# Sliding-window attention and two mixing layers on one core: the order of the weight conversion steps at the start is rearranged

## The chip, the cores and the metric

The kernel runs on one NeuronCore of a Trainium2 chip, in one launch. The core has five engines with a queue of their own: PE (TensorE, matrix products), DVE (VectorE), ACT (ScalarE), POOL (GpSimd) and SP (SyncE, which here only issues DMAs). Each works its queue in order; where an instruction waits, everything behind it on that engine waits too. The metric is the device time of one execution in microseconds.

## What is computed

Four sequences of 576 tokens, eight heads of 64. Attention looks back over 64 positions; its output goes through a gated layer (`w_in`, a product over the tokens with `w_spatial`, `w_out`) and through a second pair of layers.

```python
mask = (rel >= 0) & (rel < 64)
scores = where(mask, (q @ k.T) / 8, -1e9)
attn = softmax(scores);  x = attn @ v
h = maximum(x @ w_in, 0);  u, v = h[..., :512], h[..., 512:]
v_n = (v - mean(v)) / sqrt(var(v) + 1e-6)
gated = u * (w_spatial @ v_n + b_spatial[:, None])
x = gated @ w_out
u = x + token_mlp(x);  out = u + channel_mlp(u)
```

## The kernel before

All matrix products of the layers are made from operands split into a high and a low part (`xh`, `xl`; `wi_h`, `wi_l`), three matmuls for each pair. The weights come as 64-bit floats and are turned into 32-bit ones on the chip. A block of 128 x 512 weights takes one DMA of 512 KB into `U` (used as a landing place), one ACT step (Abs, L85 or L391) into `val`, four DVE steps (`to_f32`, L58, L60, L61, L62), one ACT step for the high part (L91 or L397) and one subtraction for the low part: on DVE (L93) for the four blocks `wv` of the second half of `w_in`, on POOL (L399) for the four blocks `wu` of its first half. These blocks are Python generators: each call `go(w)` issues the next step of that block, so that the place of a call in the text is the place of the step in the queues.

The first stage is a loop over 18 iterations (two pairs of sequences, nine tiles of 128 queries each). For tile n: `scores` (PE: mask and q·k, L201 and L206), `smax` (DVE: maxima L217 and their negative, L223, twice), `sexp` (ACT: eight exponentials, L228), `snorm` (DVE: sums to factors and one product for each half, L234, L235, L237, twice), `att_turn` (PE transposes L245, ACT copies to `PT`, L246), `att_pv` (PE, L257; ACT L265 and DVE L266 split the result to `xh`, `xl`). Then `uv_v` multiplies a tile by the second half of `w_in` (PE, L136) and `normalise` follows in turns (ACT L311, DVE L315, L316, L320, POOL L317, L318; then L296 or L288 on ACT, L297 or L289 on DVE). After every third tile four `uv_u` multiply by the first half, one block `wu` each; they are done in iteration 3 for the first time. The text of this part sets the order on every engine, by hand.

Before the loop, tile 0 and the scores of tiles 1 and 2 are interleaved with the steps of the four `wv` blocks. In the loop, `conv` says which `wu` blocks are converted in an iteration: block 0 in iteration 1, block 1 in iteration 2, blocks 2 and 3 in iteration 3. In an iteration the Abs comes behind the transposes, the DVE steps behind `att_pv`, the high part behind the maxima of tile n+2, the low part after that.

Of the kernel before, what the change touches and what calls it, by code (L numbers as in the profile page):

```python
# [29 lines left out]
def f(ap):  # L30
    return ap.bitcast(F32)
# [3 lines left out]
def tile_kernel(ctx, tc, qT, kT, kE, v, w_in, wsT, b_sp, w_out, w_t1, w_t2, w_c1, w_c2, mask, outT):  # L35
# [122 lines left out]
    def where(p, i):  # L158

        return (2 * p + (i - 1) // 4, (i - 1) % 4) if i else (None, None)  # L160

    def load_qk(n):
        p, i = its[n]
        qq = att.tile([P, 4, 128], F32, tag="qq", name="qq")
        nc.sync.dma_start(out=qq.rearrange("p j t -> p (j t)"), in_=qT[n])
        kk = att.tile([P, 4, 256], F32, tag="kk", name="kk")
        if i:
            nc.sync.dma_start(out=kk.rearrange("p j k -> p (j k)")[:, :768], in_=kT[8 * p + i - 1])
            kk = kk.rearrange("p j k -> p (j k)")[:, :768].rearrange("p (j k) -> p j k", k=192)
        else:  # L170
            nc.sync.dma_start(out=kk.rearrange("p j k -> p (j k)"), in_=kE[p])
        held[n] = (qq, kk)
# [14 lines left out]
    def scores(n):  # L187

        p, i = its[n]
        if n >= len(its):
            return
        qq, kk = held.pop(n)
        step = 64 if i else 128
        which = 1 if i and where(p, i)[1] == 0 else 0
        on_pe = n < MASK_PE
        scs = [psa.tile([P, 4, 128], F32, tag="sp", name="sc") for _ in range(2)]
        if on_pe:
            for sc in scs:  # L200
                nc.tensor.matmul(sc, ident16, msk16[:, which].unsqueeze(1).to_broadcast([P, 4, 128]), start=True, stop=False)  # L201
        for j in range(4):
            for q in range(2):
                for e in range(2):
                    er = slice(64 * e, 64 * e + 64)
                    nc.tensor.matmul(scs[e][64 * q:64 * q + 64, j, :], qq[er, j, 64 * q:64 * q + 64],  # L206
                                     kk[er, j, step * q:step * q + 128], start=not on_pe, stop=not on_pe or j == 3)
        pb = att.tile([P, 8, 128], F32, tag="pb", name="pb", bufs=3)
        nm = att.tile([P, 8], F32, tag="nm", name="nm", bufs=3)
        sm = att.tile([P, 8], F32, tag="sm", name="sm", bufs=3)  # L210
        soft[n] = (scs, pb, nm, sm, None if on_pe else msk[:, which])

    def smax(n, g):
        scs, pb, nm, sm, mk = soft[n]
        mx = att.tile([P, 4], F32, tag="mx", name="mx", bufs=3)
        if mk is None:
            nc.vector.tensor_reduce(out=mx, in_=scs[g], op=ALU.max, axis=AX.X)  # L217
        else:
            for h in range(4):
                nc.vector.tensor_tensor_reduce(  # L220
                    out=pb[:, 4 * g + h, :], in0=scs[g][:, h, :], in1=mk, scale=1.0, scalar=-3e38,
                    op0=ALU.add, op1=ALU.max, accum_out=mx[:, h:h + 1])
        nc.vector.tensor_scalar(out=nm[:, 4 * g:4 * g + 4], in0=mx, scalar1=-SCALE, scalar2=None, op0=ALU.mult)  # L223

    def sexp(n, g):
        scs, pb, nm, sm, mk = soft[n]
        for h in range(4 * g, 4 * g + 4):
            nc.scalar.activation(out=pb[:, h, :], in_=scs[g][:, h - 4 * g, :] if mk is None else pb[:, h, :],  # L228
                                 func=AF.Exp, scale=SCALE, bias=nm[:, h:h + 1], accum_out=sm[:, h:h + 1])

    def snorm(n, g):
        pb, sm = soft[n][1], soft[n][3]
        rs = att.tile([P, 4], F32, tag="rs", name="rs", bufs=4)
        nc.vector.tensor_scalar(out=rs, in0=sm[:, 4 * g:4 * g + 4], scalar1=1e-9, scalar2=None, op0=ALU.add)  # L234
        nc.vector.reciprocal(out=rs, in_=rs)  # L235
        half = pb[:, 4 * g:4 * g + 4, :]
        nc.vector.tensor_tensor(out=half, in0=half, in1=rs.unsqueeze(2).to_broadcast([P, 4, 128]), op=ALU.mult)  # L237
# [92 lines left out]
    def tick():  # L330
        for t in list(turns):
            if next(t, turns) is turns:
                turns.remove(t)
# [21 lines left out]
    def run_work(n):  # L355
        used = 0
        for _ in range(min(n, len(work))):
            fn, *a = work.pop(0)
            fn(*a)
            used += COST[fn]  # L360
        return used
# [9 lines left out]
    def wi(js, k, at):  # L371

        return split_steps(wi_h[:, k, js], wi_l[:, k, js], w_in[128 * k:128 * k + 128, js],
                           raw=U[:, k, at:at + 1024], val=stage.tile([P, 2 * WN], F32, tag="raw", name="val"))
# [9 lines left out]
    def wu_part(ft):  # L384
        fs = slice(128 * ft, 128 * ft + 128)
        raw = U[:, ft, :1024].bitcast(I32)
        val = stage.tile([P, 2 * WN], F32, tag="raw", name="val")
        nc.sync.dma_start(out=raw.rearrange("p (k c) -> p k c", k=4), in_=w_in[:, fs].rearrange("(k p) c -> p k c", p=P).bitcast(I32))
        yield
        r3 = raw.rearrange("p (n w) -> p n w", w=2)  # L390
        nc.scalar.activation(out=val, in_=f(r3[:, :, 1]), func=AF.Abs)  # L391
        yield
        to_f32(val, r3[:, :, 0], r3[:, :, 1])
        yield
        hi, lo = wi_h[:, :, fs], wi_l[:, :, fs]
        v3 = val.rearrange("p (k c) -> p k c", k=4)
        nc.scalar.copy(out=hi, in_=v3)  # L397
        yield
        nc.gpsimd.tensor_tensor(out=lo, in0=v3, in1=f(hi), op=ALU.subtract)  # L399

    E = mybir.EngineType
    with tc.manual_schedule(engines={E.PE, E.SP, E.Activation, E.DVE, E.Pool}):
        vs_ = slice(512, 1024)
        load_qk(0)
        nc.sync.dma_start(out=msk, in_=mask)
        nc.gpsimd.tensor_copy(out=msk16, in_=msk)
        wv = [wi(vs_, k, 1152) for k in range(4)]
        wu = [wu_part(ft) for ft in range(4)]

        def go(w):  # L410
            next(w, 0)

        go(wv[0])
        load_v(0)
        go(wv[1])
        load_qk(1)
        go(wv[2])
        scores(0)
        smax(0, 0)
        smax(0, 1)  # L420
        sexp(0, 0)
        go(wv[0])
        sexp(0, 1)
        go(wv[0])
        go(wv[1])
        snorm(0, 0)
        snorm(0, 1)
        go(wv[0])
        go(wv[3])
        load_v(1)  # L430
        load_qk(2)
        scores(1)
        PT = att_turn(0)
        go(wv[1])
        go(wv[0])
        go(wv[2])
        smax(1, 0)
        smax(1, 1)
        att_pv(0, PT)
        go(wv[1])  # L440
        go(wv[2])
        go(wv[1])
        go(wv[3])
        sexp(1, 0)
        go(wv[2])
        go(wv[3])
        go(wv[2])
        go(wv[3])
        go(wv[3])
        sexp(1, 1)  # L450
        go(wu[0])
        load_v(2)
        load_qk(3)
        go(wu[1])
        load_v(3)
        go(wu[2])
        go(wu[3])
        nc.sync.dma_start(out=bb, in_=bass.AP(b_sp.tensor, b_sp.offset, [[0, P], [1, S]]))
        scores(2)
        uv_v(*its[0])  # L460
        snorm(1, 0)
        snorm(1, 1)
        smax(2, 0)
        smax(2, 1)
        conv = {1: (0,), 2: (1,), 3: (2, 3)}
        ws_at = {3: 2, 4: 3, 5: 3, 6: 2}
        for n in range(1, len(its)):
            more, some = n + 2 < len(its), n + 1 < len(its)
            cv = [wu[i] for i in conv.get(n, ())]
            if more and n > 1:  # L470
                load_qk(n + 2)
                load_v(n + 2)
            PT = att_turn(n)
            for w in cv:
                go(w)
            if some:
                sexp(n + 1, 0)
                sexp(n + 1, 1)
                snorm(n + 1, 0)
                snorm(n + 1, 1)  # L480
            tick()
            left = BUDGET - run_work(1)
            att_pv(n, PT)
            for w in cv:
                go(w)
            if more:
                scores(n + 2)
                smax(n + 2, 0)
                smax(n + 2, 1)
            for w in cv:  # L490
                go(w)
            tick()
            for w in cv:
                go(w)
            while work and left > 0:
                left -= run_work(1)
                tick()
            load_ws(ws_at.get(n, 0))
            enable(n)
        while turns:  # L500
            tick()
# [242 lines left out]
```

## Time and profile before

| what | us |
|---|---|
| median of 3 runs | 690.02 |
| lowest and highest run | 688.22 and 690.04 |
| the profiled execution | 689.61 |
| its span in the trace | 687.8 |
| PE busy in the span | 651.5 (95%) |
| DVE, ACT, POOL busy | 358.4, 250.4, 21.7 |

All times in the rows are microseconds from the start of the span. "Idle before" is time in which the engine had nothing running just before an instruction, and the arrow names what ended it.

### The profile page before, as it was taken

Reading aid. Unit: us, or ns where it says so; the run is one execution under the profiler, and the core shown is the slowest. Engines: PE = TensorE matmul, PEld = TensorE weight load, DVE = VectorE, ACT = ScalarE, POOL = GpSimd, SP = SyncE. Lnnn points to the kernel's source line nnn. Section 1 sums busy time; section 2 is a strip of 40 time slices with the busy share of each in tenths; the row PEclk is TensorE's granted clock in tenths of the full one; section 3 lists DMA queues with packets and bytes.
Section 4 is the critical chain, followed back from the end, with each engine's and each line's share of the span. In section 5 each row is a group of like instructions: output and inputs, shape, how many; then the busy total and the mean of one; then the engine's idle time right before and its main releaser. Section 6 shows DMA issues by size and latency. Waiting matters only on the chain.

```text
span 687.8 us, 11757 instructions
## 1 busy us (share of the span) xinstructions
PE 651.5 (95%) x4756; PEld 615.3 (89%) x4756; DVE 358.4 (52%) x913; ACT 250.4 (36%) x675; POOL 21.7 (3%) x49
## 2 busy tenths in 40 slices
PE   3687989999999999999999999999999999999997
PEld 2455769899979999999999998999999999999997
DVE  3878687667675689952389799312212212112112
ACT  3564664552685263752353255111111111111110
POOL 0002100000100010000000000000000000000000
PEclk8689999999999999999999999999999999999999
DMA  8461455223241033200044143100100100100001
GB/s 316 128 210 50 139 170 179 73 75 127 76 139 32 2 106 116 77 1 1 1 153 123 62 155 121 47 1 0 47 1 1 46 1 7 41 1 30 17 1 46
DMA packets 28533, 50.23 MB, mean 73 GB/s; under 512 B 2496, under 2 KB 15168, under 8 KB 28480
## 3 DMA queue, kind: packets, MB, share of 16 engines
q1 hardware_dynamic: 28480, 49.49, 22.0%
q8 instruction: 37, 0.61, 0.4%
q14 instruction: 16, 0.13, 0.1%
HBM read 44.76 MB, written 4.72 MB: 72 GB/s over the span
## 4 chain that ended last, share of the span: by engine, by line
PE 81%; DVE 7%; ACT 7%; DMA 3%; issue 1%; POOL 0%; SPq 0%; DVEq 0%; ACTq 0%
PE mm L136 50%; PE A L647 21%; PE A L136 4%; ACT pb L228 4%; PE xo L257 2%; PE pt L245 2%; PE A L557 1%; ACT PT L246 1%; PE sc L206 1%; DMA raw<-in_wsT 1%; DVE pb L237 1%; DVE val L61 1%; DVE val L62 1%; DVE xl L266 1%; DVE st L315 1%
## 5 line engine op out<-in xcount | busy, mean ns | idle before, releaser
L637 DVE SCALAR_TENSOR_TENSOR g3l<-mm,g3h 128x384 fp32r<-128x384 f32 x72 | 40.0, 556 | 190.3 <-ACT g3h L636 190.1
L636 ACT ACTIVATE g3h<-mm 128x384 fp32r<-128x384 f32 x72 | 35.3, 492 | 223.1 <-PE mm L136 222.6
L136 PE MATMUL mm<-uh,c1h 128*128 128x384 f32 x288 | 97.0, 337 | 1.0 <-ACT c1h L125 1.0
L647 PE MATMUL A<-g3h,c2l 128*128 128x384 f32 x288 | 97.0, 337 | 0.0
L136 PE MATMUL mm<-uh,c1l 128*128 128x384 f32 x288 | 96.7, 336 | 0.1
L136 PE MATMUL mm<-ul,c1h 128*128 128x384 f32 x288 | 96.7, 336 | 0.0
L647 PE MATMUL A<-g3l,c2h 128*128 128x384 f32 x288 | 94.1, 337 | 0.0
L647 PE MATMUL A<-g3h,c2h 128*128 128x384 f32 x288 | 93.8, 337 | 0.0
L136 PEld LDWEIGHTS mm<-uh,c1h 128*128 128x128 f32 x288 | 54.0, 188 | 1.6 <-ACT c1h L125 1.6
L136 PEld LDWEIGHTS mm<-uh,c1l 128*128 128x128 f32 x288 | 54.0, 188 | 0.5 <-DVE c1l L126 0.5
L647 PEld LDWEIGHTS A<-g3h,c2l 128*128 128x128 f32 x288 | 54.0, 187 | 0.2
L136 PEld LDWEIGHTS mm<-ul,c1h 128*128 128x128 f32 x288 | 54.0, 188 | 0.0
L647 PEld LDWEIGHTS A<-g3h,c2h 128*128 128x128 f32 x288 | 53.7, 187 | 0.4 <-ACT c2h L125 0.3
L647 PEld LDWEIGHTS A<-g3l,c2h 128*128 128x128 f32 x288 | 53.8, 188 | 0.0
L136 PE MATMUL mm<-ws_h,nh 128*128 128x288 f32 x160 | 47.5, 301 | 0.9 <-DVE tmp L348 0.9
L136 PE MATMUL mm<-ws_l,nh 128*128 128x288 f32 x160 | 46.4, 295 | 0.0
L228 ACT ACTIVATE pb<-pb,nm 128x128 f32<-128x128 f32 x96 | 37.2, 397 | 2.6 <-DVE nm L223 2.5
L136 PE MATMUL mm<-gh,wo_h 128*128 128x288 f32 x128 | 38.0, 298 | 0.0
L136 PE MATMUL mm<-gh,wo_l 128*128 128x288 f32 x128 | 37.8, 296 | 0.0
L136 PE MATMUL mm<-ws_h,nl 128*128 128x288 f32 x128 | 37.8, 295 | 0.0
L136 PE MATMUL mm<-gl,wo_h 128*128 128x288 f32 x128 | 37.7, 295 | 0.0
L136 PE MATMUL mm<-xh,wi_h 128*128 128x384 f32 x96 | 33.4, 348 | 2.9 <-ACT wi_h L397 2.9
(118 smaller groups left out, 1339.3 us busy)
## 6 DMA issues: line engine op xcount, KB each, us to landing
wraw<-in_w_c SPq DMA_DIRECT2D x24, 512.0 KB, 3.5
kk<-in_kT SPq DMA_DIRECT2D x16, 384.0 KB, 5.0
qq<-in_qT SPq DMA_DIRECT2D x18, 256.0 KB, 4.1
va<-in_v SPq DMA_DIRECT2D x18, 256.0 KB, 2.8
vb<-in_v SPq DMA_DIRECT2D x18, 256.0 KB, 3.7
outT<-ot SPq DMA_DIRECT2D x24, 192.0 KB, 2.1
U<-in_w_in SPq DMA_DIRECT2D x8, 512.0 KB, 7.3
raw<-in_w_out SPq DMA_DIRECT2D x8, 256.0 KB, 3.3
```

The lines of the kernel that those rows point to most:

```text
L61: nc.vector.scalar_tensor_tensor(out=xi, in0=high, scalar=-0x40000000, in1=xi, op0=ALU.bitwise_and, op1=ALU.bitwise_or)
L62: nc.vector.scalar_tensor_tensor(out=xi, in0=low, scalar=29, in1=xi, op0=ALU.logical_shift_right, op1=ALU.bitwise_or)
L136: nc.tensor.matmul(o, a, c, start=(i == 0), stop=(i == n - 1))
L206: nc.tensor.matmul(scs[e][64 * q:64 * q + 64, j, :], qq[er, j, 64 * q:64 * q + 64], kk[er, j, step * q:step * q + 128], start=not on_pe, s ...
L228: nc.scalar.activation(out=pb[:, h, :], in_=scs[g][:, h - 4 * g, :] if mk is None else pb[:, h, :], func=AF.Exp, scale=SCALE, bias=nm[:, h ...
L237: nc.vector.tensor_tensor(out=half, in0=half, in1=rs.unsqueeze(2).to_broadcast([P, 4, 128]), op=ALU.mult)
L245: nc.tensor.transpose(pt[:, h, :], pb[:, 4 * g + h, :], ident)
L246: nc.scalar.copy(out=PT[:, 4 * g:4 * g + 4, :], in_=pt)
L257: nc.tensor.matmul(xo[64 * e:64 * e + 64, j, 64 * q:64 * q + 64], vt[q][:, hc], PT[:, 4 * e + j, 64 * q:64 * q + 64], start=True, stop=True)
L636: nc.scalar.activation(out=gh, in_=ps[:, :CW], func=AF.Relu)
L637: nc.vector.scalar_tensor_tensor(out=gl, in0=ps[:, :CW], scalar=0.0, in1=f(gh), op0=ALU.max, op1=ALU.subtract)
L647: nc.tensor.matmul(acc[d][:, :CW], a, c, start=(ft == 0 and i == 0), stop=(ft == 11 and i == 2))
```

## The change

The transfer of the first `wv` block is issued ahead of the first queries and keys. Its Abs, DVE steps and high part stand ahead of the first scores. The steps of the other `wv` blocks are put behind maxima and ahead of exponentials or normalisations. In the loop, blocks 1 and 2 of `wu` are converted in iteration 2 and block 3 in iteration 3; the first block of an iteration has its DVE steps ahead of the next tile's exponentials in the text (so ahead of its normalisation on DVE) and its high part behind them; the second one has its DVE steps behind `att_pv`.

```diff
+        wv = [wi(vs_, k, 1152) for k in range(4)]
+        wu = [wu_part(ft) for ft in range(4)]
+        go(wv[0])
         load_qk(0)
         nc.sync.dma_start(out=msk, in_=mask)
         nc.gpsimd.tensor_copy(out=msk16, in_=msk)
-        go(wv[0])
+        go(wv[1])
         load_v(0)
-        go(wv[1])
         load_qk(1)
         go(wv[2])
+        go(wv[3])
+        go(wv[0])
+        go(wv[0])
+        go(wv[0])
         scores(0)
         smax(0, 0)
         smax(0, 1)
+        go(wv[1])
+        go(wv[0])
         sexp(0, 0)
-        go(wv[0])
         sexp(0, 1)
-        go(wv[0])
         go(wv[1])
         snorm(0, 0)
         snorm(0, 1)
...
-        conv = {1: (0,), 2: (1,), 3: (2, 3)}
+        conv = {1: (0,), 2: (1, 2), 3: (3,)}
...
             PT = att_turn(n)
-            for w in cv:
-                go(w)
+            go(*cv)
+            go(*cv[:1])
             if some:
                 sexp(n + 1, 0)
                 sexp(n + 1, 1)
                 snorm(n + 1, 0)
                 snorm(n + 1, 1)
+            go(*cv[:1])
             tick()
             left = BUDGET - run_work(1)
             att_pv(n, PT)
-            for w in cv:
-                go(w)
+            go(*cv[:1])
+            go(*cv[1:])
+            go(*cv[1:])
             if more:
                 scores(n + 2)
                 smax(n + 2, 0)
                 smax(n + 2, 1)
-            for w in cv:
-                go(w)
             tick()
-            for w in cv:
-                go(w)
+            go(*cv[1:])
```

On ACT at the start of the program (a row with + is of the new order, with - of the old one, without a sign of both; L85 is an Abs of a `wv` block, L91 its high part, L228 an exponential, L246 the copy of `PT`):

```order
-L228 ACT_TABLE_LOAD
+L85 ACT_TABLE_LOAD
+L85 ACTIVATE val<-U 128x512
+L91 CAST wi_h<-val 128x512
+L85 ACTIVATE val<-U 128x512
+L228 ACTIVATE pb,sm<-sc,nm 128x128 x8
+L85 ACTIVATE val<-U 128x512
+L91 CAST wi_h<-val 128x512
+L246 COPY PT<-pt 128x512 x2
+L85 ACTIVATE val<-U 128x512
 L228 ACTIVATE pb,sm<-sc,nm 128x128 x4
```

The table load stands first, and two Abs stand ahead of the first exponentials, which are eight in a row now; before, the load stood with the exponentials and one Abs between their halves.

On DVE at the start, the rows behind the first block's four steps (maxima of tile 0, the first block's low part, the second block's four steps):

```order
+L217 TENSOR_REDUCE mx<-sc 128x4
+L223 TENSOR_SCALAR nm<-mx 128x4
+L217 TENSOR_REDUCE mx<-sc 128x4
+L223 TENSOR_SCALAR nm<-mx 128x4
+L93 TENSOR_TENSOR wi_l<-val,wi_h 128x512
 L58 TENSOR_SCALAR val<-val 128x512
 L60 TENSOR_SCALAR val<-val 128x512
 L61 SCALAR_TENSOR_TENSOR val<-U,val 128x512
 L62 SCALAR_TENSOR_TENSOR val<-U,val 128x512
```

These four steps stood behind the normalisation of tile 0; they now stand ahead of it.

On DVE in iteration 1 (L58 to L62 convert `wu` block 0; L234, L235, L237 normalise tile 2):

```order
-L320 TENSOR_SCALAR vf<-vf,mv,rstd 128x512
-L266 TENSOR_TENSOR xl<-xo,xh 128x4x128
 L58 TENSOR_SCALAR val<-val 128x512
 L60 TENSOR_SCALAR val<-val 128x512
 L61 SCALAR_TENSOR_TENSOR val<-U,val 128x512
 L62 SCALAR_TENSOR_TENSOR val<-U,val 128x512
+L234 TENSOR_SCALAR rs<-sm 128x4
+L235 RECIPROCAL rs<-rs 128x4
+L237 TENSOR_TENSOR pb<-pb,rs 128x512
+L234 TENSOR_SCALAR rs<-sm 128x4
+L235 RECIPROCAL rs<-rs 128x4
+L237 TENSOR_TENSOR pb<-pb,rs 128x512
```

The conversion has moved from behind `xl` to ahead of the normalisation.

On ACT in iterations 2 and 3 (L391 is an Abs of a `wu` block, L397 its high part, L311 and L265 as above):

```order
+L391 ACTIVATE val<-U 128x512 x2
+L228 ACTIVATE pb,sm<-sc,nm 128x128 x8
+L397 CAST wi_h<-val 128x4x128
+L311 ACTIVATE vf<-mm 128x512
+L265 CAST xh<-xo 128x4x128
+L397 CAST wi_h<-val 128x4x128
+L246 COPY PT<-pt 128x512 x2
 L391 ACTIVATE val<-U 128x512
 L228 ACTIVATE pb,sm<-sc,nm 128x128 x8
-L311 ACTIVATE vf<-mm 128x512
-L265 CAST xh<-xo 128x4x128
-L397 CAST wi_h<-val 128x4x128
```

Iteration 2 has two Abs and two high parts now, and the second high part stands ahead of the copies of iteration 3; one block is left for iteration 3. PE's order is the same in both programs.

## Rows read from the trace of the kernel before

**Rows 1.** The page, part 1: busy time, share, instructions.

```profile
PE 651.5 (95%) x4756; PEld 615.3 (89%) x4756; DVE 358.4 (52%) x913; ACT 250.4 (36%) x675; POOL 21.7 (3%) x49
```

**Rows 2.** Stretches, L136 alone: length, PE busy (count), PEld, PEclk, DMA, GB/s.

```profile
58.80:63.00 4.20, 4.20 (x24) 4.09 (x24) 1.00 0.40 140
67.46:71.30 3.84, 3.84 (x13) 3.84 (x14) 0.56 0.70 201
71.40:73.10 1.70, 1.70 (x10) 1.42 (x9) 1.00 0.03 13
```

**Rows 3.** Timeline, iteration 3: start, duration, engine, operation, [idle before, releaser].

```profile
66.11 0.44 PE L136 MATMUL mm<-xh,wi_h 128*128 128x384 f32 x1 [2.90 <-ACT wi_h L397]
66.13 1.27 POOL L399 TENSOR_TENSOR wi_l<-val,wi_h 128x512 fp32r<-128x512 f32 x1 [2.59 <-ACT wi_h L397]
66.24 1.72 DVE L61 SCALAR_TENSOR_TENSOR val<-U,val 128x512 int32<-128x512 int32 x1
67.46 0.44 PE L136 MATMUL mm<-xh,wi_l 128*128 128x384 f32 x1 [0.73 <-POOL wi_l L399]
```

**Rows 4.** Timeline, start of the program (all engines but PE).

```profile
5.34 0.40 POOL L406 CAST msk<-msk 128x256 bf16<-128x256 f32 x1 [3.69 <-DMA msk<-in_mask]
8.77 0.69 DVE L217 TENSOR_REDUCE mx<-sc 128x4 f32<-128x512 f32 x1 [8.77 <-PE sc L206]
9.74 1.28 ACT L228 ACT_TABLE_LOAD   x1 [9.74 <-DVE nm L223]
13.12 0.43 DVE L58 TENSOR_SCALAR val<-val 128x512 f32<-128x512 f32 x1 [2.66 <-ACT val L85]
15.38 0.16 DVE L234 TENSOR_SCALAR rs<-sm 128x4 f32<-128x4 f32 x1
17.41 0.42 DVE L58 TENSOR_SCALAR val<-val 128x512 f32<-128x512 f32 x1
22.03 0.69 DVE L266 TENSOR_TENSOR xl<-xo,xh 128x512 fp32r<-128x512 f32 x1
27.74 1.46 DVE L93 TENSOR_TENSOR wi_l<-val,wi_h 128x512 fp32r<-128x512 f32 x2
```

**Rows 5.** DMA, the issue at 2.10 alone (first `wv` block): count, KB, us to landing.

```profile
U<-in_w_in SPq DMA_DIRECT2D x1, 512.0 KB, 6.6
```

**Rows 6.** A stretch: PE, PEld, DVE, ACT, POOL busy, PEclk, DMA, GB/s.

```profile
11.00:12.00 1.00, 0.00 (x0) 0.00 (x0) 0.00 (x0) 0.99 (x7) 0.00 (x0) 1.00 1.06 431
```

**Rows 7.** DMA, first issue from 38.12 on alone (block 2 of `wu`).

```profile
U<-in_w_in SPq DMA_DIRECT2D x1, 512.0 KB, 6.0
```

**Rows 8.** Timeline, iterations 1 and 2, DVE, ACT and POOL.

```profile
35.32 0.67 ACT L391 ACTIVATE val<-U 128x512 f32<-128x512 f32 x1
37.41 0.17 DVE L234 TENSOR_SCALAR rs<-sm 128x4 f32<-128x4 f32 x1 [2.24 <-ACT pb L228]
38.62 0.63 ACT L265 CAST xh<-xo 128x512 fp32r<-128x512 f32 x1
39.84 0.54 DVE L320 TENSOR_SCALAR vf<-vf,mv,rstd 128x512 f32<-128x512 f32 x1
43.26 0.62 ACT L397 CAST wi_h<-val 128x512 fp32r<-128x512 f32 x1 [4.00 <-DVE val L62]
43.95 1.26 POOL L399 TENSOR_TENSOR wi_l<-val,wi_h 128x512 fp32r<-128x512 f32 x1 [10.97 <-ACT wi_h L397]
44.65 0.59 DVE L223 TENSOR_SCALAR nm<-mx 128x4 f32<-128x4 f32 x1
45.06 1.07 ACT L246 COPY PT<-pt 128x512 f32<-128x512 f32 x2
50.71 0.69 DVE L315 BATCH_NORM_STATS2 st<-vf 128x6 f32<-128x512 f32 x1
52.10 0.42 DVE L58 TENSOR_SCALAR val<-val 128x512 f32<-128x512 f32 x1
54.99 1.06 ACT L246 COPY PT<-pt 128x512 f32<-128x512 f32 x2
```

More of the change, by code (lines that the diff above doesn't have):

```diff
@@ L403, in tile_kernel, with go @@
         vs_ = slice(512, 1024)
+        wv = [wi(vs_, k, 1152) for k in range(4)]
+        wu = [wu_part(ft) for ft in range(4)]
+        def go(*ws):
+            for w in ws:
+                next(w, 0)
+        go(wv[0])
         load_qk(0)
@@ L406, in tile_kernel @@
         nc.gpsimd.tensor_copy(out=msk16, in_=msk)
[L407 to L411, printed above, removed]
-        go(wv[0])
+        go(wv[1])
         load_v(0)
-        go(wv[1])
         load_qk(1)
         go(wv[2])
+        go(wv[3])
+        go(wv[0])
+        go(wv[0])
+        go(wv[0])
         scores(0)
@@ L427, in tile_kernel @@
         snorm(0, 1)
-        go(wv[0])
-        go(wv[3])
+        go(wv[2])
+        go(wv[1])
         load_v(1)
         load_qk(2)
+        go(wu[0])
         scores(1)
         PT = att_turn(0)
-        go(wv[1])
-        go(wv[0])
-        go(wv[2])
         smax(1, 0)
         smax(1, 1)
+        go(wv[2])
+        go(wv[3])
+        sexp(1, 0)
         att_pv(0, PT)
@@ L441, in tile_kernel @@
         go(wv[2])
[L442 to L445, printed above, removed]
         go(wv[3])
         go(wv[2])
+        sexp(1, 1)
         go(wv[3])
         go(wv[3])
-        sexp(1, 1)
-        go(wu[0])
         load_v(2)
```

## The prediction, made before the changed kernel ran

> **What bounds the kernel now.** I read the page first: PE is busy for 651.5 of 687.8 us [rows 1], so a change that leaves PE's work and its order alone can win at most the 36 us in which PE waits, and what PE loses at its lower clock. The stretches of PE and the timeline say where that is: before about 75 us, in the part that this change rearranges. The largest wait there stands in iteration 3. PE runs the first two `uv_u` at 4.20/24 = 0.175 us a matmul with a granted clock of 1.00 (the upper level, 2.4 GHz), then waits 2.90 us for the high part of `wu` block 2 and 0.73 us for its low part [rows 2, 3]. Behind that wait the granted clock is 0.56 for 3.84 us, mostly the lower level of 1.2 GHz, in which 13 matmuls take 0.295 us each; then it is 1.00 again, with ten in 1.70 us [rows 2]. The waits and the slow matmuls belong together. The last `uv_u` ends at about 73.1, so the question is how early the four `uv_u` end. Ahead of them DVE sets the pace: it converts weights and normalises with few pauses from 13.12 on.
>
> **The start.** The mask's landing releases the first scores now (its cast at 5.34, the first maximum at 8.77) [rows 4]. With the 512 KB block in front, the mask becomes the last of the same four transfers of which the block is the last now, landing at 2.10 + 6.6 = 8.7 [rows 5]. As a lower bound, 512 KB at the 431 GB/s of an undisturbed stretch take 1.2 us [rows 6], so 6.5. I take 8.7, whose row is of these very four, and keep 6.5 for the range. The first maximum then moves by 8.7 - 5.3 = 3.4 us, to 12.2.
>
> Against that stand three savings. The table load of 1.28 us waited for the first negative maxima [rows 4]; it stands first on ACT now, with nothing to wait for. DVE's 2.66 us of idle time ahead of its first conversion go, since at 12.2 work is waiting. And that conversion, 15.38 - 13.12 = 2.26 us, lies ahead of the first maximum, under the transfers. From 8.77 to the last steps on `wv` at 27.74 DVE takes 18.97 us; less 2.66 and 2.26 that is 14.05, which from 12.2 gives 26.25. One wait is new. `xl` comes 22.03 - 15.38 = 6.65 us behind the start of the normalisation (through transposes, `PT`, `att_pv`). The normalisation starts at 12.2 + 2.2 (the maxima and one subtraction: what is left of 22.03 - 17.41 after a conversion, less a small wait) + 2.26, so `xl` at 23.3; DVE gets there some 0.7 us earlier. That makes 26.95: the start gains 0.8 us.
>
> **Iteration 1.** All is 0.8 earlier. The conversion of block 0 moves into DVE's 2.24 us of idle time ahead of the normalisation of tile 2 [rows 8]. Its Abs ends at about 35.9 - 0.8 = 35.1, so the normalisation starts at 37.35 where 36.6 would have done; its first half takes 1.0 and ends at 38.4. By then ACT, behind the last exponential (38.62 - 0.8 = 37.8), makes the high part, and POOL starts its L399 0.69 later (43.95 - 43.26), at 38.5, for 1.27 us [rows 8].
>
> Here is a cost that the diff does not show. Where L399 met DVE in the old order, DVE's instruction stood still until L399 ended: L223 took 0.59 instead of 0.17, L61 1.72 instead of its usual 0.69 [rows 3, 8]. In the new order L399 meets the second half of a normalisation, three instructions on SBUF. That costs nothing if they slip through, 1.2 us if they stand until 39.8; both observed collisions say the second, so the half ends at 40.6 instead of 39.4. The Trainium skill ("SBUF — State Buffer", section "Who interferes with whom") says that DVE and GpSimd share a port pair as an exclusive lock: a DVE instruction with two SBUF inputs, or in a two-port mode, and a GpSimd one that reads SBUF shut each other out, whichever starts first running to its end. L61's 1.72 agrees with it. By that rule the reciprocal (0.2) could pass, and the two collisions that I count would take 0.4 less: 682.9.
>
> L320 and `xl` (1.05), the maxima (1.6) and L297 (two of 0.7, like L266 [rows 4]) follow without the conversion between them: 44.6. ACT, which stands behind the high part until 43.26 now, starts the copies of `PT` for tile 2 at 42.3 (L320, then two casts) instead of 45.06 [rows 8].
>
> **Iteration 2.** Block 1 converts while the exponentials run: 44.6 to 46.85. The normalisation's first half takes 1.0, the second meets L399 again (in the same place as in iteration 1) and ends at 50.1. Then 52.10 - 50.71 = 1.4 to the next conversion, at 51.5 instead of 52.10 [rows 8]. So the copies for tile 3 start at 54.4 instead of 54.99: 0.6 is left. Block 2's transfer lands now at 38.12 + 6.0 = 44.1 [rows 7], 0.8 earlier then; its Abs comes at about 43.9 and just finds it.
>
> **Iteration 3.** `uv_u` starts 0.6 earlier too, at 58.2. Block 2 is ready. Block 3 follows the maxima (done at 55.6) and L320 on DVE, 56.1 to 58.4; its high part stands behind the exponentials, and L399 ends by 61. Its matmuls come up at 58.2 + 36 x 0.175 = 64.5: covered by 3.5 us. 48 matmuls at 0.175 and 0.2 for the last one's end make 8.6 us: 66.8, against 73.1. In terms: 0.6 + 3.6 (both waits) + 2.1 (24 matmuls in 6.3 us now, 4.2 then) = 6.3 us. Nothing behind it is altered: PE's queue, ACT's chain, and the DMAs, which are issued as buffers come free, move along.
>
> So 689.6 - 6.3 = 683.3 us. The sum is made against the profiled execution (689.61, span 687.8); the median 690.02 lies 0.4 above that, inside what the three runs differ by.
>
> **Rivals.**
> - More is won. If L399 holds no instruction of DVE, neither half is 1.2 late, and the gain is 6.3 + 2.4 = 8.7: 680.9. For it: one POOL instruction has to get in between many short ones. Against it: L399 held DVE in both rows. If the mask lands at 6.5, that gives 2.2 as well: 681.1. Both together 678.7. Chance 0.27 for either.
> - A wait for a block comes back. "u weights in the second iteration" is true of two blocks of four only; block 3 stays in iteration 3, and PE waits again if DVE gets to it 3.5 us late. Or block 2's transfer lands late, with next to no cover: ACT then holds the exponentials of tile 3 behind its Abs. If half of the 5.7 us returns, 686.2; 685 to 688. Chance 0.14.
> - Slower: PE's lower clock, in the `uv_u` of iteration 3 and the `uv_v` behind them. PE waits less there, but is still partly idle ahead of them, and its clock did fall after a wait. Taking the full-speed part out of the 3.84 us, a matmul costs 0.325 at the lower level, 0.15 more. All 48 cost 7.2 us, the twelve longer ones of `uv_v` at least 1.8: 692.3. It decides from 42 slow matmuls (6.3/0.15), some 13.7 us at a stretch. Against it: the one after the present wait lasted under 3.84, and 58.80 to 63.00 has 1.00 [rows 2]. Chance 0.05.
> - No change: something behind iteration 3 keeps its old time, and PE waits there instead. Against it: each transfer of the loop is issued behind a PE step that moves. 689 to 690. Chance 0.04.
>
> **How the numbers follow.** The forecast, with 681.3 to 685 as its own range, has 0.50; the rivals as given. A difference under 0.3% (2.1 us) is about what a measurement of this kernel can't tell from no change. Faster by more than that are the forecast, the first rival and most of the second: 0.87. Within it 0.08, slower 0.05. To hold the time 8 times in 10 the range takes in the first rival but for its end and half of the second: 679.2 to 686.5.
>
> **What would show it.** Right: a table load within the first 2 us; the first maximum near 12; copies of `PT` for tiles 2 and 3 near 42.3 and 54.4; DVE instructions of a normalisation that last over 1 us beside L399; four `uv_u` with no wait for `wi_h`, ending near 67; and the same distance kept in all later stages. Wrong in the start, if the first maximum is late and the last steps on `wv` are not before 27.7; wrong in the collision, if `uv_u` ends by 65; wrong in the whole, if PE waits for block 3, or if the gain at 73 is gone at 120.

## The result and the profile after

| | before | after |
|---|---|---|
| median of 4 runs each, us | 689.87 | 681.99 |
| lowest and highest run | 688.22, 690.04 | 681.54, 683.86 |
| profiled execution, its span | 689.61, 687.8 | 682.27, 680.2 |

The ratio is 0.9896, with a 95% interval of 0.9872 to 0.9920. The change makes the kernel 1.0% faster; forecast were 683.3 us, with 679.2 to 686.5 as the range. A second comparison of the same two programs gave 681.65 us and 0.9867 (0.9840 to 0.9895).

The page, part 1, of the kernel after (against [rows 1]):

```profile
PE 649.1 (95%) x4756; PEld 613.8 (90%) x4756; DVE 359.0 (53%) x913; ACT 250.6 (37%) x675; POOL 21.7 (3%) x49
```

The counts are the old ones; PE is 2.4 us less busy, and the span is 7.6 us shorter. So some 5 us of the gain are waits that are gone.

**The start.** The timeline of the kernel after, ACT, DVE and POOL, in order of time (against [rows 4]; L414 is the mask's cast that stood on L406):

```profile
0.72 1.28 ACT L85 ACT_TABLE_LOAD   x1 [0.72 <-PEq L731]
5.76 0.43 DVE L58 TENSOR_SCALAR val<-val 128x512 f32<-128x512 f32 x1 [5.76 <-ACT val L85]
7.95 0.41 POOL L414 CAST msk<-msk 128x256 bf16<-128x256 f32 x1 [6.30 <-DMA msk<-in_mask]
11.39 0.69 DVE L217 TENSOR_REDUCE mx<-sc 128x4 f32<-128x512 f32 x1 [3.29 <-PE sc L206]
15.84 0.16 DVE L234 TENSOR_SCALAR rs<-sm 128x4 f32<-128x4 f32 x1
22.49 0.69 DVE L266 TENSOR_TENSOR xl<-xo,xh 128x512 fp32r<-128x512 f32 x1 [0.69 <-ACT xh L265]
25.95 1.46 DVE L93 TENSOR_TENSOR wi_l<-val,wi_h 128x512 fp32r<-128x512 f32 x2
```

The table load runs under the transfers. The first conversion runs from 5.76, also under them, and DVE still waits 3.29 us for the mask's way to the first maximum. From there on it has work without a pause but for the 0.69 us at `xl`. The last steps on `wv` stand at 25.95 instead of 27.74: 1.8 us earlier.

**Iterations 1 and 2.** The same timeline, DVE, ACT and POOL (against [rows 8]):

```profile
36.84 0.69 DVE L237 TENSOR_TENSOR pb<-pb,rs 128x512 f32<-128x512 f32 x1
37.51 1.27 POOL L399 TENSOR_TENSOR wi_l<-val,wi_h 128x512 fp32r<-128x512 f32 x1 [6.32 <-ACT wi_h L397]
37.65 0.18 DVE L235 RECIPROCAL rs<-rs 128x4 f32<-128x4 f32 x1
37.86 1.48 DVE L237 TENSOR_TENSOR pb<-pb,rs 128x512 f32<-128x512 f32 x1
41.11 1.07 ACT L246 COPY PT<-pt 128x512 f32<-128x512 f32 x2
46.08 0.66 ACT L397 CAST wi_h<-val 128x512 fp32r<-128x512 f32 x1
48.74 0.22 POOL L317 TENSOR_SCALAR rstd<-mv 128x1 f32<-128x1 f32 x1 [9.96 <-DVE mv L316]
49.05 0.57 POOL L318 TENSOR_TENSOR rstd<-rstd,mhalf 128x1 f32<-128x1 f32 x1
49.59 1.29 POOL L399 TENSOR_TENSOR wi_l<-val,wi_h 128x512 fp32r<-128x512 f32 x1
49.60 1.56 DVE L60 TENSOR_SCALAR val<-val 128x512 int32<-128x512 int32 x1
52.65 0.62 ACT L397 CAST wi_h<-val 128x512 fp32r<-128x512 f32 x1 [4.94 <-DVE val L62]
53.17 1.07 ACT L246 COPY PT<-pt 128x512 f32<-128x512 f32 x2
53.33 0.68 DVE L217 TENSOR_REDUCE mx<-sc 128x4 f32<-128x512 f32 x1
53.34 1.27 POOL L399 TENSOR_TENSOR wi_l<-val,wi_h 128x512 fp32r<-128x512 f32 x1 [2.47 <-ACT wi_h L397]
54.05 0.59 DVE L223 TENSOR_SCALAR nm<-mx 128x4 f32<-128x4 f32 x1
```

Read each L399 with the DVE instruction that overlaps it. The first holds the second L237 (1.48 where the first L237 took 0.69, so 0.8 lost), but lets the reciprocal at 37.65 through. The second stands behind L317 and L318 in POOL's queue, of which L317 waits for DVE; it starts at 49.59 and holds L60 of the next block (1.56 where L60 takes 0.43 elsewhere, so 1.1 lost). The third lets the maximum through and holds the small L223. The copies for tiles 2 and 3 stand at 41.11 and 53.17, forecast at 42.3 and 54.4.

**Iteration 3.** PE's timeline, the first and the last matmul of the four `uv_u` of the kernel after:

```profile
58.25 0.67 PE L136 MATMUL mm<-xh,wi_h 128*128 128x384 f32 x1
66.74 0.34 PE L136 MATMUL mm<-xh,wi_l 128*128 128x384 f32 x1
```

The same two of the kernel before:

```profile
58.76 0.44 PE L136 MATMUL mm<-xh,wi_h 128*128 128x384 f32 x1
72.80 0.33 PE L136 MATMUL mm<-xh,wi_l 128*128 128x384 f32 x1
```

After, no wait stands in the 48 rows from one to the other; the last ends at 67.08, where it ended at 73.13. L136 alone, as in [rows 2]:

```profile
58.80:67.00 8.20, 8.20 (x48) 7.96 (x46) 1.00 0.37 132
```

So the waits of 2.90 and 0.73 us are gone [rows 3], and with them the slow matmuls behind them. But the clock fell elsewhere. A stretch of the kernel after, all engines (PE, PEld, DVE, ACT, POOL busy, PEclk, DMA, GB/s):

```profile
55.36:58.77 3.41, 3.41 (x38) 2.24 (x37) 3.17 (x10) 3.41 (x17) 0.00 (x0) 0.50 0.58 112
```

It holds the scores of tile 5 and the first `uv_u` matmuls. In the kernel before, a stretch of about that length holds the same scores, with `att_pv` in front of them:

```profile
55.62:58.83 3.21, 3.05 (x67) 2.25 (x67) 1.42 (x4) 3.21 (x13) 0.81 (x1) 1.00 0.19 34
```

After, the stretch ran at the lower level (0.50 of 2.4 GHz is 1.2 GHz); the scores and the first `uv_u` matmuls took longer. `att_pv` of tile 3 starts at 53.80 where it was 55.62, 1.8 earlier, while `uv_u` starts at 58.25 where it was 58.76: 4.45 us from the one to the other instead of 3.14. So 1.3 us of the lead went to the clock.

**Behind it.** The lead stays near 6 us up to 85 us and then grows at `att_pv` of tile 6. There PE waits in the kernel before (and no longer after) for the copies of `PT`, which stand in ACT's queue behind three splits of `w_spatial` rows (ACT and PE, kernel before):

```profile
90.81 0.43 ACT L91 CAST ws_h<-raw 128x288 fp32r<-128x288 f32 x1 [1.61 <-DMA raw<-in_wsT]
92.32 0.43 ACT L91 CAST ws_h<-raw 128x288 fp32r<-128x288 f32 x1 [1.08 <-DMA raw<-in_wsT]
93.30 0.43 ACT L91 CAST ws_h<-raw 128x288 fp32r<-128x288 f32 x1 [0.55 <-DMA raw<-in_wsT]
94.28 0.33 PE L257 MATMUL xo<-PT,va 128*64 128x64 f32 x2 [0.79 <-ACT PT L246]
```

ACT's same instructions after:

```profile
84.70 1.33 ACT L91 CAST ws_h<-raw 128x288 fp32r<-128x288 f32 x3 [1.36 <-DMA raw<-in_wsT]
```

ACT waits 1.36 instead of 3.24 us (1.61 + 1.08 + 0.55) for those transfers. SP issues them behind the last values (`vb`); before:

```profile
86.19 1.76 SPq L181 DMA_DIRECT2D vb<-in_v  x1
88.05 1.32 SPq L75 DMA_DIRECT2D raw<-in_wsT  x3
```

And after:

```profile
80.34 0.38 SPq L181 DMA_DIRECT2D vb<-in_v  x1
80.82 1.32 SPq L75 DMA_DIRECT2D raw<-in_wsT  x3
```

One issue took 1.4 us less, and the transfers behind it started 7.2 instead of 5.8 us earlier. The start of `att_pv` of tile 7, before and after:

```profile
110.00 0.34 PE L257 MATMUL xo<-PT,va 128*64 128x64 f32 x4
102.77 0.34 PE L257 MATMUL xo<-PT,va 128*64 128x64 f32 x4
```

So 7.2 us are left there, and 7.6 at the end.

### The profile page after: what moved, and what is told of

It reads as the page before. It is cut to its first block, busy times and chain, and to the rows that moved or that the text cites. A ratio compares the mean times of both kernels' runs of the same rounds, so it can differ in the third digit from the quotient of the medians.

```text
span 680.2 us, 11755 instructions
## 1 busy us (share of the span) xinstructions
PE 649.1 (95%) x4756; PEld 613.8 (90%) x4756; DVE 359.0 (53%) x913; ACT 250.6 (37%) x675; POOL 21.7 (3%) x49
## 4 chain that ended last, share of the span: by engine, by line
PE 83%; DVE 8%; ACT 5%; DMA 3%; issue 1%; SPq 1%; DVEq 0%; POOL 0%; ACTq 0%
PE mm L136 51%; PE A L647 22%; PE A L136 4%; ACT pb L228 3%; PE xo L257 2%; PE sc L206 1%; DVE pb L237 1%; PE A L557 1%; ACT PT L246 1%; PE pt L245 1%; DMA raw<-in_wsT 1%; DMA msk<-in_mask 1%; DVE val L61 1%; DVE val L62 1%; DMA raw<-in_w_out 1%
## 5 line engine op out<-in xcount | busy, mean ns | idle before, releaser
L136 PE MATMUL mm<-uh,c1h 128*128 128x384 f32 x288 | 97.0, 337 | 1.0 <-ACT c1h L125 1.0
L136 PE MATMUL mm<-uh,c1l 128*128 128x384 f32 x288 | 96.7, 336 | 0.1
L136 PE MATMUL mm<-ul,c1h 128*128 128x384 f32 x288 | 96.7, 336 | 0.0
L136 PEld LDWEIGHTS mm<-uh,c1h 128*128 128x128 f32 x288 | 54.0, 188 | 1.6 <-ACT c1h L125 1.6
L136 PEld LDWEIGHTS mm<-uh,c1l 128*128 128x128 f32 x288 | 54.0, 188 | 0.5 <-DVE c1l L126 0.5
L136 PEld LDWEIGHTS mm<-ul,c1h 128*128 128x128 f32 x288 | 54.0, 188 | 0.0
L136 PE MATMUL mm<-ws_h,nh 128*128 128x288 f32 x160 | 47.5, 301 | 0.9 <-DVE tmp L348 0.9
L136 PE MATMUL mm<-ws_l,nh 128*128 128x288 f32 x160 | 46.4, 295 | 0.0
L228 ACT ACTIVATE pb<-pb,nm 128x128 f32<-128x128 f32 x96 | 37.2, 396 | 2.6 <-DVE nm L223 2.5
L136 PE MATMUL mm<-gh,wo_h 128*128 128x288 f32 x128 | 38.0, 298 | 0.0
L136 PE MATMUL mm<-gh,wo_l 128*128 128x288 f32 x128 | 37.8, 296 | 0.0
L136 PE MATMUL mm<-ws_h,nl 128*128 128x288 f32 x128 | 37.8, 295 | 0.0
L136 PE MATMUL mm<-gl,wo_h 128*128 128x288 f32 x128 | 37.7, 295 | 0.0
L136 PE MATMUL mm<-xh,wi_h 128*128 128x384 f32 x96 | 32.9, 342 | 0.0
```

What stands on the lines that cost most here:

```text
L136: nc.tensor.matmul(o, a, c, start=(i == 0), stop=(i == n - 1))
```

## The experiments

Ratios are to the kernel before, run on the same chip beside the experiment.

**start_only.** The new start with the old loop: everything ahead of `conv` from the kernel after, the loop from the kernel before.

```
 (start of after, up to scores(2) ... smax(2, 1))
 conv = {1: (0,), 2: (1,), 3: (2, 3)}
 (loop of before)
```

> The steps ahead of the loop in the new order, the loop and its table of blocks as before. Theory (the parts add, the wait of iteration 3 is the larger one): the last steps on wv at about 26 instead of 27.7, everything in the loop 1.8 us earlier, PE still waits some 2.9 us for the high part of block 2 and 0.7 us for its low part in iteration 3; 687.5 to 688.5 us. Rival (the start is absorbed by DVE's idle 2.24 us in iteration 1): same time as before within 0.5 us.

Measured: 687.84 us, ratio 0.9953 (0.9940 to 0.9967). PE, iteration 3:

```profile
64.33 0.45 PE L136 MATMUL mm<-xh,wi_h 128*128 128x384 f32 x1 [2.92 <-ACT wi_h L397]
65.68 0.69 PE L136 MATMUL mm<-xh,wi_l 128*128 128x384 f32 x1 [0.73 <-POOL wi_l L399]
```

The two waits are whole and stand 1.8 earlier; the last `uv_u` ends at 71.3, 1.8 earlier. The start is worth 1.8 us in the trace (one execution; the ratio would make it 2.3 to 4.1) and removes no wait of the loop.

**loop_only.** The old start with the new loop (the table and the places).

```
 (start of before)
 conv = {1: (0,), 2: (1, 2), 3: (3,)}
 (loop of after)
```

> The steps ahead of the loop as before, the loop and its table of blocks in the new order. Theory: copies of PT for tile 1 at 33.8 as before, no wait for wi_h in iteration 3, the last uv_u ends near 69; 683.5 to 685 us. Rival (the new loop needs the early start, since block 2's transfer lands at 44 and ACT waits for it with the exponentials behind): 686 us or more, with an idle time of ACT in front of an L391.

Measured: 684.31 us, ratio 0.9908 (0.9892 to 0.9924). `uv_u` runs without a wait from 59.99 to 68.58, 4.55 earlier than before. By the medians the two parts add up: 2.7 + 6.2 = 8.9, against 7.9 and 9.0 in the two comparisons. By the traces they do too, 1.8 + 4.55 = 6.35 against 6.05 of both together, but that is partly chance. The copies for tile 1, up to which the program is that of before, came at 35.01 and not at 33.8 as expected: from 28.68 to 31.20 the granted clock was 0.50 in this execution, where the same five matmuls of the kernel before had 1.00. These 1.2 us are missing in the 4.55, and the 1.3 us of lower clock above are missing in the 6.05; in after_again (below), without that stretch, `uv_u` ends 7.7 earlier than before.

**conv_only.** The kernel before with the new table alone, the places as they were.

```diff
-        conv = {1: (0,), 2: (1,), 3: (2, 3)}
+        conv = {1: (0,), 2: (1, 2), 3: (3,)}
```

> Only the table is changed (block 2 in iteration 2 instead of 3), every step in its old place. Theory (the place of the steps matters as much as the iteration): both conversions stand ahead of the maxima and both high parts ahead of the copies of PT, so these start near 57.5 instead of 55, uv_u starts near 61, and block 3 comes just late for the last uv_u; end near 70.5, 686 to 688 us. Rival (the table alone is the whole gain of the loop): 683 to 684.5 us.

Measured: 689.98 us, ratio 1.0002 (0.9989 to 1.0014): no change, where I had expected a part of the gain. ACT, end of iteration 2:

```profile
59.76 0.62 ACT L397 CAST wi_h<-val 128x512 fp32r<-128x512 f32 x1 [2.66 <-DVE val L62]
60.28 1.07 ACT L246 COPY PT<-pt 128x512 f32<-128x512 f32 x2
```

With both blocks in the old places the high part of the second waits for DVE and holds the copies for tile 3 until 60.28 (54.99 before). `uv_u` has no wait inside, but starts at 65.36 and ends at 74.2, 1.1 later than before. What was saved in iteration 3 is spent in iteration 2. A part of the late end is the clock and not the table: the copies for tile 1, ahead of any change, came 1.4 late in this execution (35.22 instead of 33.82), and from 62.25 to 65.36 the granted clock was 0.54. That nothing is gained rests on the eleven runs. The direction was expected, the size was not.

**place_only.** The kernel after with the old table: the new places alone.

```diff
-        conv = {1: (0,), 2: (1, 2), 3: (3,)}
+        conv = {1: (0,), 2: (1,), 3: (2, 3)}
```

> The changed kernel with the table of before (blocks 2 and 3 both in iteration 3); every step's place as in the changed kernel. Theory (the places of the steps made the loop's gain, not the earlier iteration; block 2 in iteration 2 even holds the copies of PT for tile 3 by its DVE steps): these copies start near 48 instead of 52.7, uv_u starts near 55, PE waits 1.5 us or less for block 3, the last uv_u ends at 64 to 65.5 instead of 67.1; 679 to 680.5 us. Rival (the earlier iteration took the wait away): PE waits 2.5 us or more for block 3, the end is at 68 or later; 683.5 us or more.

Measured: 681.42 us, ratio 0.9874 (0.9858 to 0.9891), the time of the kernel after and later than I had expected. ACT's copies for tile 3:

```profile
48.19 1.07 ACT L246 COPY PT<-pt 128x512 f32<-128x512 f32 x2 [0.77 <-PE pt L245]
```

PE's waits in `uv_u`:

```profile
60.10 0.44 PE L136 MATMUL mm<-xh,wi_l 128*128 128x384 f32 x1 [0.88 <-POOL wi_l L399]
62.94 0.45 PE L136 MATMUL mm<-xh,wi_h 128*128 128x384 f32 x1 [0.81 <-ACT U L283]
63.84 0.44 PE L136 MATMUL mm<-xh,wi_l 128*128 128x384 f32 x1 [0.28 <-POOL wi_l L399]
```

The copies come 5 us earlier, `uv_u` starts at 54.43, 3.8 us earlier than in the kernel after, and has waits of 2.0 us in it again (the 0.81 is for L283, which empties a product and stands behind block 3's high part in ACT's queue); it ends at 65.84. With the places changed, the iteration in which block 2 is converted makes no difference to the time that these runs show. start_only is the same program with the old places: 687.84 against 681.42 us. So conv_only, start_only and place_only together answer the question which edit of the loop acts: the places.

**qk_first.** The kernel after with queries, keys and mask issued ahead of the first weight block again.

```diff
-        go(wv[0])
         load_qk(0)
         nc.sync.dma_start(out=msk, in_=mask)
         nc.gpsimd.tensor_copy(out=msk16, in_=msk)
+        go(wv[0])
```

> The changed kernel with the first queries, keys and the mask issued ahead of the first weight block again; all other steps as in the changed kernel. Theory (the first maxima wait behind the first block's DVE steps in any case, so that the order of the two transfers hardly matters): the mask lands near 5.3, the block near 8.7, its conversion ends at 11.6 and the first maximum comes then instead of at 11.4; within 0.4 us of the changed kernel. Rival (the early transfer is what the start gains by): the last steps on wv 1 us or more later, 683 us or more.

Measured: 681.65 us, ratio 0.9880 (0.9858 to 0.9902), not different from the kernel after. DVE at the start:

```profile
9.41 0.43 DVE L58 TENSOR_SCALAR val<-val 128x512 f32<-128x512 f32 x1 [9.41 <-ACT val L85]
...
11.67 0.68 DVE L217 TENSOR_REDUCE mx<-sc 128x4 f32<-128x512 f32 x1
```

The mask is there at 5.3 again, but the conversion stands ahead of the maxima in DVE's order and now waits for its own transfer, so that the first maximum comes at 11.67 instead of 11.39, and the last steps on `wv` at 26.04 instead of 25.95. Which of the two is transferred first makes 0.1 to 0.3 us; the start's gain comes from the order of the steps.

**low_dve.** The kernel after with the low part of `wu` on DVE: no POOL instruction beside the conversions.

```diff
-        nc.gpsimd.tensor_tensor(out=lo, in0=v3, in1=f(hi), op=ALU.subtract)
+        nc.vector.tensor_tensor(out=lo, in0=v3, in1=f(hi), op=ALU.subtract)
```

> The changed kernel with the four low parts of the wu blocks (L399) computed by DVE in the same places of the text, none by POOL. Theory (DVE instructions stand still while POOL's L399 runs): no instruction of a normalisation or a conversion over 0.8 us in iterations 1 to 3; ahead of the copies of PT for tile 3 DVE saves 0.8 + 1.1 us and pays two subtractions of 0.6, so these start near 52.5 instead of 53.2, and the time falls by some 0.7 us. Rival (the long instructions have another cause): they stay, and the time rises by 1.2 us.

Measured: 680.82 us, ratio 0.9867 (0.9849 to 0.9884). DVE, the instructions that had been held:

```profile
37.86 0.69 DVE L237 TENSOR_TENSOR pb<-pb,rs 128x512 f32<-128x512 f32 x1
50.03 0.43 DVE L60 TENSOR_SCALAR val<-val 128x512 int32<-128x512 int32 x1
53.34 0.17 DVE L223 TENSOR_SCALAR nm<-mx 128x4 f32<-128x4 f32 x1
```

Without L399 on POOL all three have their usual length, at the same places in the order. That DVE stood still because of it is shown. DVE pays 0.68 for each low part instead, so that `att_pv` of tile 3 comes 0.7 earlier (53.10). In the medians nothing is shown of it: the ratio is that of the second comparison of the kernel after.

**pe_fill.** The kernel after with nine more matmuls, whose product is overwritten, ahead of `att_pv` of tile 3, where PE waits 1.95 us for ACT's copies.

```diff
+        for _ in range({3: 9}.get(n, 0)):
+            nc.tensor.matmul(xo..., wi_h[:, 0, 512:640], wi_h[:, 0, 512:], start=True, stop=True)
```

> The changed kernel with nine extra matmuls of 512 columns (result overwritten) on PE in iteration 3, ahead of att_pv, where PE waits 1.95 us for the copies of PT. Theory (the lower clock of the scores and the first uv_u of iteration 3 comes from PE's wait just ahead of them): granted clock 1.00 from 54 to 67, the scores of tile 5 in 1.7 us instead of 2.9, uv_u ends 1.2 us earlier, and the time falls by about 1 us. Rival (the lower clock comes from the partly idle time before that, or falls anywhere): a stretch at the lower level remains, no gain, or 0.2 us lost where the extra matmuls run over.

Measured: 681.52 us, ratio 0.9874 (0.9856 to 0.9892), as the kernel after. The stretch of `att_pv` and the scores:

```profile
55.20:58.10 2.90, 2.90 (x69) 2.07 (x67) 2.73 (x7) 2.90 (x16) 0.00 (x0) 1.00 0.16 47
```

The clock is at the upper level there, but in this execution the lower stretch lay earlier (46.8 to 50.2), so that the nine matmuls came late and ended only at 55.4. It can't be said whether they did anything for the clock. Inconclusive as to the clock; no gain in time.

**wv1_early.** The kernel after with the second `wv` block converted ahead of the first maxima.

```diff
         scores(0)
+        go(wv[1])
+        go(wv[0])
+        go(wv[1])
         smax(0, 0)
         smax(0, 1)
-        go(wv[1])
-        go(wv[0])
         sexp(0, 0)
         sexp(0, 1)
-        go(wv[1])
```

> The changed kernel with the four DVE steps of the second wv block and the low part of the first one ahead of the first maxima, in DVE's idle 3.29 us. Theory (DVE's pace sets the start): its block lands at 9.2, conversion 9.8 to 12.05, first maximum 0.7 us later, the normalisation of tile 0 done 1.0 us earlier, last steps on wv at 25.0 instead of 25.95; about 1 us faster. Rival (the first maxima set the start): 0.7 us later throughout, no gain.

Measured: 681.25 us, ratio 0.9869 (0.9851 to 0.9887). The conversion fills DVE from 10.01 to 12.27, the first maximum moves from 11.39 to 12.27, and the last `wv` steps come at 25.29 instead of 25.95: 0.66, where 1.0 was expected. Alone too small to be told in the median.

**two and three.** two is wv1_early and low_dve together; three has the old table besides.

```diff
-        conv = {1: (0,), 2: (1, 2), 3: (3,)}
+        conv = {1: (0,), 2: (1,), 3: (2, 3)}
```

> The changed kernel with both: the second wv block's steps ahead of the first maxima, and the four L399 on DVE. Theory (each shortens the same chain of DVE by 0.7 us ahead of the copies of PT for tile 3): these at 51.3 instead of 52.65; 680 to 681 us. Rival (one takes the other's slack): as one of them alone.

> Both edits and the table of before. Theory: 1.4 us less than with that table alone, so 677.5 to 679.5 us. Rival (PE or a transfer sets the pace there by then, for instance the keys of tile 4): no less than with the table alone.

Measured: two 680.30 us, ratio 0.9857 (0.9842 to 0.9872), the lowest median of all. three 681.36 us, ratio 0.9872 (0.9854 to 0.9890), later than expected: as in place_only `uv_u` starts earlier (55.02) but waits 0.93 us for block 3's low part, and nothing is left of it at the end. No version was shown to be faster than the kernel after: two lies 0.1 to 0.4% below it by the ratios to the kernel before, and the intervals overlap with that of the second comparison.

**before_again and after_again.** Both programs unchanged, once more, to see what differs between executions of one program.

> The kernel before, once more, for a second trace: where its stages stand against the first trace tells how much of a difference of 1 us between two traces is the chip's own. Theory: up to 75 us the same within 0.5 us; behind that stretches at the lower clock may lie elsewhere and move the later stages by up to 1 us. 689 to 691 us.

> The changed kernel once more, for a second trace and more runs. Theory (where the lower clock falls differs from execution to execution, and only its place decides what it costs): up to the copies of PT for tile 3 (52.65) the same within 0.5 us; if the stretch at the lower level doesn't lie on the scores and first uv_u of iteration 3, the last uv_u ends near 65.7 instead of 67.1. Rival (the program alone fixes it): the lower level from 55.4 to 58.8 again, end at 67.1. 681 to 683 us.

Measured: before_again 689.31 us in its one run, with `att_pv` of tiles 2 to 6 within 0.9 us of the first execution and the last within 0.2. The 0.9 stands at tile 3 (56.50 instead of 55.62), where I had expected 0.5 at most. after_again 681.65 us. Its stretch beside the one above of the kernel after:

```profile
55.36:58.77 3.41, 3.41 (x45) 2.83 (x44) 3.20 (x9) 3.41 (x16) 0.00 (x0) 1.00 0.56 165
```

The same program, the copies for tile 3 within 0.13 us of the same time (53.04; the 52.65 of the expectation is the high part just ahead of them), and the upper level throughout this stretch; `uv_u` starts at 56.80 instead of 58.25, and the next `att_pv` at 68.97 instead of 70.62. So the lower clock in that stretch belongs to the execution, or to the chip it ran on, and not to the order of the program; which chip the first execution had is not on record. But of these 1.65 us only 0.46 are left at `att_pv` of tile 7 and 0.4 at the end. SP in after_again:

```profile
78.81 1.69 SPq L181 DMA_DIRECT2D vb<-in_v  x1
80.60 1.32 SPq L75 DMA_DIRECT2D raw<-in_wsT  x3
```

The issue of `vb` took 1.69 us in this execution, as it did before the change, so that the `w_spatial` rows were issued at 80.60, only 0.2 earlier than in the other execution. PE caught up with them and waited at `att_pv` of tile 6 (0.47 us), as in the kernel before.

## Why the prediction was right, and where its steps were not

**What bounds the kernel: right.** The gain lies ahead of 100 us, most of it in the four `uv_u` of iteration 3. start_only keeps both waits, loop_only has neither.

**The start: right in kind, one term mis-sized.** Forecast 0.8, measured 1.8 (start_only: 1.8 as well). The step that failed is the mask's landing: I took 8.7 from the row of a 512 KB block that came last of four transfers; the mask, of 128 KB in the same place, is cast at 7.95. The first maximum follows at 11.39 instead of 12.2. From there to the last `wv` steps the sum held: 25.95 - 11.39 = 14.6, against the forecast's 26.95 - 12.2 = 14.75, and its new wait at `xl` of 0.7 is the 0.69 in the row. So 0.8 of the 1.0 us missed is the mask.

**The collision of L399 with the normalisation: right in block 0, wrong in block 1.** In block 0 an instruction stood still as forecast, for 0.8 and not 1.2 us, since the reciprocal passed. The Trainium skill ("SBUF — State Buffer", section "Who interferes with whom") says that a DVE instruction with two SBUF inputs, or in a two-port mode, and a GpSimd one that reads SBUF shut each other out, and that a `tensor_reduce` never contends; the rows at 37.65 (reciprocal, 0.18), 37.86 (two inputs, held) and 53.33 (reduction, 0.68) agree; whether L60 and L223, with one input, ran in such a mode is shown by no row. In block 1 the step "meets L399 again (in the same place as in iteration 1)" failed. I had looked at DVE's and ACT's queues and not at POOL's: L317 and L318 of iteration 2 stand ahead of L399 there, and L317 waits for DVE's statistics, so that L399 starts at 49.59 and not right behind its high part (ACT L397 at 46.08, 0.66 long). It cost nearly the same (1.1), in the conversion of block 2 instead.

**Start and end of `uv_u`: right by two errors that cancel.** Forecast 58.2 and 66.8, measured 58.25 and 67.08. The copies for tile 3 came at 53.17, 1.2 ahead of the forecast (the start's 1.0 and the smaller collision's 0.4 would make 1.4; 0.2 were lost on the way), and the lower clock of 55.36 to 58.77 took 1.3. In after_again, without that stretch, `uv_u` starts at 56.80, where the forecast without both errors would have put it (58.2 - 1.2 = 57.0). What the prediction says of the clock was that it falls behind PE's waits; that its place changes between executions of one program was not in it. The rival with 42 slow matmuls did not come: in 58.80 to 67.00 all 48 are at 1.00.

**"Nothing behind it is altered": wrong by 1.6 us.** The lead grew from 6.0 to 7.2 in iteration 6 and to 7.6 at the end. The profiled executions differ by 689.61 - 682.27 = 7.3, forecast 6.3. What sets the lead there is the issue of the `w_spatial` rows, for which PE waits where it comes late. It stood at 88.05 before, and at 80.82 and 80.60 in the two executions after: 7.2 and 7.45 earlier, and the leads at `att_pv` of tile 7 are 7.2 and 7.7, though those of tile 4 were 6.05 and 7.7. The short issue of `vb` (0.38 instead of 1.76) gave the first execution what the clock had taken; in the second one the clock took nothing and the issue was long (1.69). So executions whose `uv_u` ended 1.7 us apart (67.08 and 65.42) differ by 0.4 in the end. This is read from the traces and was not tried by an experiment of its own; nor is the last 0.4 of the 7.6 us explained. The fourteen traces of this case bear it out: none of the seven in which that issue took 0.38 us has a wait at `att_pv` of tile 6; of the seven in which it took 1.5 to 1.8, five have one of 0.15 to 0.79 us, and the other two (before_again, start_only) have a stretch at the lower clock just ahead instead.

**The rivals.** That L399 holds nothing is refuted by low_dve beside the rows after, though the time came half-way to that rival through the mask and the late 1.6 us. The wait for block 3 or block 2 did not come. The clock did cost something, but 1.3 us and not the 9.0 of that rival (692.3 - 683.3). "No change" fell with the first trace.

**What the change's words say.** "u weights done in the second iteration" and "first weight block transferred ahead" are not where the gain is: place_only and qk_first, which undo them, have the time of the kernel after. The places of the steps carry it, at the start and in the loop. Which of the moved steps carries most in the loop, DVE's four or ACT's high part, which stood ahead of the copies, was not separated. The prediction had both in its terms, but it took the 3.6 us of waits as gone because block 2 is converted an iteration earlier ("Block 2 is ready"), and did not ask which edit could be left out.

## What to carry to other kernels

Where an engine converts weights beside a latency chain, look for its idle time ahead of an instruction of the chain and put the conversion there; moving it to an earlier iteration without such a place gained nothing here (conv_only). When a step is moved, follow it in every queue it enters: the POOL instruction met another DVE instruction than forecast because of two small ones ahead of it in its own queue. And when a gain comes before a transfer that has its own pace, read how early that transfer can be issued before counting the gain at the end.

## What the runs showed of the hardware that was not expected

- Instructions of DVE stand still beside POOL's L399, even ones of four elements a partition: L223 took 0.59 and 1.04 (at 54.05 and 62.01) instead of 0.17, L60 1.56 instead of 0.43, L237 1.48 instead of 0.69; a reduction from PSUM and a reciprocal did not.
- The place of a stretch at the lower clock differs between executions of the same program: 55.36 to 58.77 was at 0.50 in one execution of the kernel after and at 1.00 in the other. It was worth 1.3 to 1.5 us at that place. All fourteen traces have a lower stretch between about 30 and 38; a second one, between 45 and 59, stands in ten of them at different places and in four (after_again, loop_only, low_dve, place_only) not at all. Behind the two waits of `uv_u` it fell in all three traces that have them (before, before_again, start_only).
- The same DMA issue on SP (`vb`, 256 KB, at about 80 us) took 0.38 us in one execution of the kernel after and 1.69 in another, and delayed the issues behind it. Of the fourteen traces seven have 0.38 and seven 1.52 to 1.81. Why is open: no run was made for it.
